# Slot 5's q and k turned by DMA instead of on TensorE, in a fused retention and feed-forward kernel

## The chip, the cores and the metric

The kernel runs on one core of one Trainium2 chip. The metric is the device time of one launch in microseconds. Engines: PE is TensorE (matmuls; PEld its weight loads), DVE is VectorE, ACT is ScalarE, POOL is GpSimd, SP is SyncE. SP and POOL issue DMAs here: POOL through a software queue (q0 in the profile), SP through a hardware queue (q1). Both queues run on the core's same 16 DMA engines.

## The reference

```python
# q, k, v: (4 batches, 8 heads, 768 steps, 64)
gamma = 1.0 - 2.0 ** (-5.0 - np.arange(H, dtype=np.float32))
for t in range(S):
    state = gamma[None, :, None, None] * state + np.einsum('bhd,bhe->bhde', k[:, :, t], v[:, :, t])
    y[:, :, t] = scale * np.einsum('bhd,bhde->bhe', q[:, :, t], state)
# x: y with heads beside each other, 3072 tokens x 512
h = x @ w_in                      # 512 -> 2048
out = (h * np.cos(h)) @ w_out     # 2048 -> 512
```

A linear recurrence with a decay for each head is followed by a feed-forward layer whose activation is h cos h. Inputs and output are float32; the matmuls run in bfloat16.

## The kernel before

**Tiles.** Time is cut into six chunks of 128 steps and the batches into two pairs, which gives 12 *slots* (`NP`), each one chunk of one batch pair, 256 tokens. Two slots make a *group* of 512 tokens for the feed-forward layer. For a slot the recurrence becomes matrix work:

1. q and k are cast to bfloat16 and multiplied by decay factors (`conv_q`, `conv_k`, `conv_v`: L323 to L346; for most slots q on POOL, k on ACT, v on POOL or DVE).
2. q and k are *transposed*, so that head dimension lies on the partitions (tile `qkt`, three buffers, slot p uses buffer p % 3).
3. Scores: k times q (`a_mm`/`a_one`, PE, L392), masked on DVE (`a_mask`, L411) into `am`.
4. Outputs: scores times v plus q times the running state; and the state's update (`y_block`, PE lines L483, L497, L511). From slot 4 on the scores of slot p+1 are woven into the block of slot p ("block 4" holds slot 4's outputs and slot 5's scores). Such a block takes six of the seven PSUM banks.
5. `y_copy` brings the outputs to `xt`, the feed-forward input; `s_copy` the state to `stb`.

The feed-forward layer comes in units of 4 or 8 matmuls, some 0.87 us of PE each: *half units* (`h_mm`, L614: 256 tokens, two column tiles of w_in), *full units* (`f_mm`, L593: 512 tokens, one column tile), each followed by a cosine on ACT (`f_cos`, L601) and a multiply on DVE (L605, L622), which frees the unit's bank; and *w_out units* (`o_mm`, L638), four of which make one 128-token output tile, copied by `o_out` and stored by SP.

**Transposes, two ways.** `t_mm` (L358 to L366) transposes on PE: for one slot 16 matmuls against an identity (L364), in two halves u, into PSUM; four copies (`t_copy`, L316 on ACT or L318 on DVE) bring them to `qkt`. `dma_t` (L351 to L353) does it with two DMA transposes on SP, q and k, 256 KB each, straight from `qs` and `ks` to `qkt`, without PE, PSUM or a copy. `DMA_T = 6` (L197) sets the border: slots 0 to 5 on PE, slots 6 and up by DMA.

**What sets the order.** Everything up to slot 6 is ordered by a planner at build time (class `Plan`). Each operation has a list of allowed engines, a cost, operations it comes after, and a rank; the planner goes through time, gives each free engine the ready operation of lowest rank, and so writes one fixed instruction order for each engine. It keeps counts of banks, cosine buffers, and a `port` token: POOL's two-input operations and some casts of DVE may not run at once. It models the loads as one queue (`mb`, `rate`, `lag`). The dictionary `SHIFT` adds to ranks and `ON` fixes engines, operation by operation (L168, L169); both come from a search. Where PE has nothing ready in the first 18 us, the planner inserts filler matmuls on zeros (`idle_mm`, L667). The plan's times only make the order: in the program each engine goes through its list and waits only for data and buffers. After slot 6 the order is a loop written out by hand.

The planner's entry for the DMA transposes stands at L803:

```python
            for w, x in enumerate("qk"):
                T["dt", p, w] = add("S", (1.3, 4.6), lambda e, p=p, w=w: dma_t(p, w),
                                    [T["c" + x, p, 0], T["c" + x, p, 1], ld["k", 7, 0]] + old, 10 * p,
                                    name="dt%d%d" % (p, w))
```

`ld["k", 7, 0]` is the load of slot 7's k, the last but one on POOL's queue: the plan places no DMA transpose before it has landed. `old` are the earlier users of the `qkt` buffer.

**Loads.** POOL issues, in a fixed list (`LOADS`), q, k and v of slots 1 to 7 (512 KB each; q4 is slot 4's q), the weights w_in in pieces (w0A to w3b) and w_out in four parts (o0 to o3, 1 MB read each). Slot 0's q goes over SP. From slot 8 on SP loads all. The order from q4 on: q4, o2, k4, v4, q5, k5, o3, v5, q6, k6, v6, q7, k7, v7.

Of the kernel before, what the change touches and what calls it, by code (L numbers as in the profile page):

```python
# [28 lines left out]
class Plan:  # L29
# [35 lines left out]
    def run(self, start, cold_until=0.0, look=0.0, fill=None, hold=""):  # L65
# [6 lines left out]
        t = 0.0  # L72
        while left:
            nxt = []
            for e in "SPADE":
# [6 lines left out]
                for op in left:  # L82
                    if e not in op["engines"]:
                        continue
                    r = self.ready(op)
                    if r is None:
                        continue
                    if r > t + 1e-9:
                        nxt.append(r)
                        coming.append((r, op["rank"]))  # L90
                        if op["rank"] < 20:
                            soon = min(soon, r)
                        continue
                    ok = True
                    for k, n in op["take"]:
                        tk = sorted(self.tokens[k])
                        n += op["spare"] if k == "bank" else 0
                        if len(tk) < n:
                            ok = False
                            continue  # L100

                        at = max(tk[n - 1] - 0.5, tk[n - 3]) if n > 5 else tk[n - 1]
                        if at > t + 1e-9:
                            nxt.append(at)
                            ok = False
                    if not ok:
                        continue
                    key = (op["rank"] + (0.5 if op["mode"] and op["mode"] != mode[0] else 0), op["n"])
                    if best is None or key < best[0]:
                        best = (key, op)  # L110
# [28 lines left out]
                for k, n in op["take"]:  # L139
                    self.tokens[k].sort()  # L140
                    del self.tokens[k][:n]
                op.update(eng=e, start=t, free=t + busy, done=t + took, lat=self.LAT[e])
                free[e] = t + busy
                if op["mb"]:
                    self.dma = max(self.dma, t + busy + 1.6) + op["mb"] / op["rate"] + op["lag"]
                    op.update(done=self.dma + 0.9, lat=0.0)
                for k, n in op["give"]:
                    self.tokens[k] += [op["done"] + 0.052] * n
# [19 lines left out]
SHIFT = {"ml010": 25.5, "mulf0.2": -74.7, "f0.3": 0.3, "cosf0.2": -11.6, "cosf0.3": -2.2, "mulf0.3": -4.9, "f0.2": 2.8, "m011": -20.0, "mulh1.4": -20.5, "m000": 82.7, "cosf0.5": -41.6, "ck21": 45.1, "a31": -124.5, "m100": 2.2, "f0.5": 23.0, "a5": -2.5, "v0": -97.2, "ms110": 6.4, "ml110": -41.8, "cosf0.4": -0.9, "f0.4": -9.8, "mulf0.5": 16.9, "eq51": 13.1, "m110": 64.4, "t20": -21.1, "k5": -46.0, "mulf0.8": 31.6, "yc21": -50.4, "f0.6": 2.1, "f0.7": 55.3, "ek10": -92.1, "w0b": -22.2, "a21": -34.2, "h1.0": 81.4, "cosh2.2": 3.0, "m501": 38.5, "yc30": -23.3, "ml011": -27.8, "mulf0.15": 5.8, "sc5": 79.1, "m201": -81.3, "mulh2.2": -18.0, "oc1": -45.8, "mulf0.14": -66.8, "cq31": -32.2, "mulf0.9": -47.9, "mulf0.6": 5.7, "cosf0.7": -27.8, "a30": -8.1, "cosf0.6": -7.2, "h0.2": -12.1, "eq21": -4.6, "cq51": 3.2, "cq41": 38.6, "f0.14": 23.8, "ek20": -13.4, "yc50": 39.8, "cv51": 23.4, "ek51": 88.5, "mulh2.10": 23.3, "cq70": 8.6, "f0.10": -46.0, "mulf0.13": 1.5, "h1.6": 5.9, "ml100": 20.1, "f0.15": 60.8, "o2.1": -8.1, "h3.10": 31.9, "t51": 14.8, "h3.0": -7.1, "h3.14": 28.8, "cq00": -2.7, "m601": 4.7, "h1.4": 1.8, "eq11": 37.0, "cosf0.12": -60.7, "v6": -26.4, "m400": 17.7, "mulh3.12": 67.0, "w2": 49.4, "sw": -53.6, "cv10": -0.0, "rv00": 14.5, "mulh2.8": 4.5, "ek50": 72.2, "cosf0.11": 2.4, "m101": -34.4, "h2.2": 1.1, "q2": -22.9, "q5": -59.7, "cosh3.14": 19.9, "y3": 19.8, "t40": 30.7, "o2": -0.8, "mulh3.4": -0.3, "cq40": -13.2, "mulh0.2": -29.3, "y5": -35.7, "mulh3.14": -25.5, "h2.12": -50.9, "oc0": -94.2, "a10": 39.9, "ek11": -35.3, "h0.6": 6.9, "eq40": -6.2, "h2.6": 58.1, "rv10": -9.1, "dt71": -1.3, "cosh3.8": -31.0, "cosh0.2": 18.8, "cv70": -67.6, "o3.1": -13.8, "cq60": -11.1, "ck60": 71.1, "m511": 10.9, "sc4": -15.9, "o1.3": -16.8, "m510": 4.5, "k4": 12.5, "h0.4": -9.2, "cq71": 3.6, "mulh3.2": 58.9, "cosh1.2": -26.7, "mulh3.6": -1.4, "cv61": 13.7, "o2.2": -9.8, "q6": -7.4, "o0.2": -7.5, "mulh2.4": 44.5, "mulh2.6": 22.6, "mulh3.10": 16.6, "v5": -53.7, "cq61": 27.8, "o1.1": -27.2, "ck61": 0.2, "m200": -10.8, "cosf0.9": 6.3, "cosh0.4": 11.6, "q4": 78.9, "cosh3.6": -6.8, "h1.2": -87.9, "tq01": 1.8, "oc3": -74.8, "mulh0.0": -16.9, "eq01": 11.2, "t21": 6.2, "ck41": 29.7, "cosh3.4": 9.3, "oc2": 8.6, "m211": 23.9, "cq01": -56.9, "w0a": 17.8, "o1.0": -7.7, "yc01": 2.2, "k7": 54.8, "yc51": -0.7, "cosf0.13": -14.9, "cosh2.10": -36.4, "yc00": 7.1, "cosh1.4": -13.4, "ek00": -8.7, "m611": -13.9, "tk10": -101.4, "mulh0.4": -40.7, "mulf0.10": 15.2, "m600": -35.2, "a00": -17.4, "cosh2.0": -5.5, "m301": 18.6, "rv11": -50.0, "sc0": -52.0, "ek01": -31.6, "cv01": 13.3, "ek21": -3.2, "cosf0.10": 7.2, "v7": -2.1, "ek40": 18.1, "t31": 22.7, "mulh1.6": 0.2, "eq30": -9.4, "y4": 19.2, "tk11": 1.9, "ek31": -26.9, "w3b": 23.5, "cosh2.12": -0.2, "cosh0.6": 4.7, "cosh2.8": -4.4, "cosh3.2": 25.8, "cv60": 2.7, "cosh2.4": -14.4, "v4": -1.1, "mulh2.12": 36.6, "dt61": -8.8, "eq41": -12.5, "mulf0.11": 31.8, "ek41": -0.8, "eq50": 9.1, "a11": -23.9, "yc10": 9.3, "o0.3": 0.3, "dt60": -3.3, "o3.3": 50.5, "mulh2.14": -42.3, "m610": -12.1, "f0.11": -0.6, "s0": 3.1, "cv11": 38.9, "h3.8": -17.4, "yc40": 14.3, "m410": -8.4, "h2.8": -4.0, "m300": 15.8, "o0": -14.6, "cv31": -27.4, "rv01": 0.6, "cosf0.14": 2.4, "cosh2.6": 11.7, "cv50": -6.8, "m010": -1.2, "ms011": -12.0, "f0.13": -5.2, "l8": 5.1, "ck70": 3.2, "t41": 1.0, "o1.2": -2.3, "cv71": 0.5, "tq11": 31.2, "h2.4": -3.6, "mulh0.6": 8.8, "t50": 7.1, "ck31": 42.7, "yc20": -52.3, "m001": -4.7, "y01": 62.0, "y2": 15.3, "f0.12": 20.5, "ms111": 2.0, "mulh1.2": -13.9, "cosh3.10": -49.0, "ck51": -9.0, "h0.0": -0.1, "eq31": 1.4, "eq20": -5.1, "q7": 1.5, "cosh3.0": 6.2, "cosh3.12": 1.5, "cv40": 2.3, "y11": 3.6, "o1": -24.4, "cv00": -1.4, "sc2": -3.2, "m411": 18.0, "m210": -8.1, "v3": 0.0, "eq10": 1.1, "tk01": 22.8, "yc41": -25.6, "cq21": -1.8, "f0.9": -31.4}  # L168
ON = {"cv70": "P", "cv00": "D", "cv30": "D", "cv31": "D", "cv60": "D", "cv11": "D", "cv10": "P", "rv01": "D", "sc5": "D", "rv11": "A", "yc20": "D", "sc3": "D", "eq40": "DA", "eq50": "A", "rv00": "A", "yc00": "D", "yc31": "DA", "ek51": "D", "ek11": "DA", "sc4": "D", "ek20": "A", "cv61": "P", "eq01": "DA", "cv51": "D", "ek41": "D", "eq41": "A", "cv20": "P", "yc01": "DA", "eq20": "A", "eq30": "DA", "ek50": "D", "ek00": "D", "sc2": "DA", "yc50": "DA", "yc40": "A", "yc21": "A", "cq21": "D", "ek40": "DA", "cv01": "D", "cv71": "P", "cv21": "P", "ek21": "DA", "cv41": "P", "cq20": "D", "ek10": "DA", "yc30": "A", "ek01": "D"}  # L169
# [4 lines left out]
def kernel(  # L174
# [22 lines left out]
    DMA_T = 6  # L197
# [515 lines left out]
    plan = Plan({"bank": 7, "cos": 3, "sem": 8, "out": 4, "port": 1, "ring": 7}, 6.5)  # L713
# [7 lines left out]
    ld["q", 0, 0], ld["q", 0, 1], ld["k", 0, 0], ld["k", 0, 1] = map(at, (3.9, 5.0, 7.4, 7.4))  # L721
    LOADS = ["Q1", "K1", "v0", "v1", "w0A", "w0B", "w0b", "w1a", "w1b", "w2", "q2", "k2", "w3a", "v2", "w3b", "o0", "q3", "k3", "v3", "o1", "q4", "o2", "k4", "v4", "q5", "k5", "o3", "v5", "q6", "k6", "v6", "q7", "k7", "v7"]
    LAG = {"w1b": 0.15}
    pend = []
    for i, x in enumerate(LOADS):
        if x[0] in "qkvQK":
# [3 lines left out]
                    [("sem", 1), ("ring", 1)], [("sem", 1), ("ring", 1)], mb=524288e-6, rate=330e-3, name=x)  # L730
# [3 lines left out]
        elif x[0] == "w":  # L734
# [4 lines left out]
                    mb=n * 2048e-6, rate=(415e-3 if n > 256 else 390e-3 if n > 128 else 370e-3),  # L739
# [3 lines left out]
        else:  # L743
            r = int(x[1])
            o = add("P", 0.76, lambda e, r=r: load_w_out(r), [("issued", prev)], 50 + i,
                    [("sem", 1)], [("sem", 1)], mb=1048576e-6, rate=415e-3, name=x)
# [4 lines left out]
    for p in range(PL + 2):  # L751
# [48 lines left out]
        else:  # L800
            for w, x in enumerate("qk"):
                T["dt", p, w] = add("S", (1.3, 4.6), lambda e, p=p, w=w: dma_t(p, w),
                                    [T["c" + x, p, 0], T["c" + x, p, 1], ld["k", 7, 0]] + old, 10 * p,  # L803
                                    name="dt%d%d" % (p, w))
# [115 lines left out]
    plan.run({"S": 2.5, "P": 3.2, "A": 5.5, "D": 3.6, "E": 4.2}, COLD, 0.6, (4.2, 18.0, 0.225, lambda e: idle_mm(e, 2)), HOLD)  # L920
# [80 lines left out]
```

## Time and profile before

| | |
|---|---|
| median of 3 runs | 208.82 us (208.31 to 208.92) |
| span of the profiled execution, first to last instruction | 206.6 us |
| the profiled execution's own device time | not listed; the median is 2.2 us above the span |
| PE matmuls | 201.9 us busy, 2179 instructions |
| DVE, ACT, POOL busy | 112.9, 115.1, 75.2 us |
| 16 transposes of slot 5 on PE (L364) | from 55.38 us, 0.89 us in the chain |
| filler matmuls (L667) | 35, 11.2 us |
| first DMA transpose issued on SP | 62.56 us |
| landing after issue of the 12 DMA transposes | 2.7 / 2.8 / 4.4 us (min, median, max) |

Times in the text are microseconds from the span's start. PE time is modelled from the ends of pipelined matmuls. The chain of work that ended last is followed back from the end: what is in it set the time. A load's landing is counted from the start of its issue. Of the software queue's loads, these matter below (start of issue, landing after it, and so the time of landing):

| load | issued | lands after | at |
|---|---|---|---|
| w_out part o0 | 21.47 | 11.1 | 32.57 |
| k5 | 36.38 | 13.9 | 50.28 |
| k6 | 45.18 | 12.1 | 57.28 |
| k7 | 50.76 | 11.0 | 61.76 |
| v7 (the last) | 51.95 | 11.4 | 63.35 |

### The profile page before, as it was taken

What the parts mean: (1) busy time and instruction counts of PE and PEld (TensorE: products, weight loads), DVE (VectorE), ACT (ScalarE), POOL (GpSimd) and SP (SyncE); (2) the same over time, 40 slices, a digit from 0 to 9 for tenths busy, and PEclk for the clock granted to TensorE, in tenths of its full rate; (3) what the DMA queues carried; (4) which work ended last, traced back from release to release, by engine and by line L of the source; (5) the groups of instructions that cost most, each with busy time, mean ns of one, the idle gap of its engine ahead of it and who ended that gap; (6) DMA issues with size and microseconds to landing.
All of it is one profiled execution on the core that took longest, in us unless ns stands there. A gap on an engine that the chain in (4) does not pass through costs nothing.

```text
span 206.6 us, 5235 instructions
## 1 busy us (share of the span) xinstructions
PE 201.9 (98%) x2179; PEld 108.9 (53%) x2179; DVE 112.9 (55%) x194; ACT 115.1 (56%) x193; POOL 75.2 (36%) x79
## 2 busy tenths in 40 slices
PE   7999999999999999999999999999999999999994
PEld 2547665868945545445445445445444444444442
DVE  5477899776787548338438438448442444444000
ACT  7566794859965357547547546554555553554120
POOL 8899989799985003305206105200000000000000
PEclk9999999999999999999999999999999999999999
DMA  6999999999999865886876975501101101110212
GB/s 117 172 264 201 304 242 322 252 333 278 341 332 190 199 156 150 206 210 155 190 183 157 144 198 147 156 0 56 53 1 51 51 3 51 51 51 0 105 52 102
DMA packets 59656, 32.15 MB, mean 156 GB/s; under 512 B 48752, under 2 KB 54128, under 8 KB 59632
## 3 DMA queue, kind: packets, MB, share of 16 engines
q0 software_dynamic: 15408, 15.47, 34.6%
q1 hardware_dynamic: 44080, 16.28, 31.7%
q8 instruction: 17, 0.28, 0.6%
q10 hardware_dynamic: 144, 0.07, 0.1%
q14 instruction: 7, 0.06, 0.1%
HBM read 27.26 MB, written 6.29 MB: 162 GB/s over the span
## 4 chain that ended last, share of the span: by engine, by line
PE 93%; DMA 4%; POOL 1%; issue 0%; DVE 0%; POOLq 0%; DVEq 0%
PE bank L638 39%; PE bank L593 30%; PE bank L614 10%; DMA kx<-in_k_dram 4%; PE bank L392 2%; PE bank L483 2%; PE bank L364 2%; PE bank L658 2%; PE st_ps L511 2%; PE bank L667 2%; PE bank L497 1%; POOL ks L284 1%; PE bank L434 1%; POOL qs L284 1%; PE bank L402 0%
## 5 line engine op out<-in xcount | busy, mean ns | idle before, releaser
L601 ACT ACTIVATE cosb<-bank,halfpi 128x512 bf16<-128x512 f32 x96 | 65.6, 689 | 54.1 <-PE bank L593 47.8
L638 PE MATMUL bank<-w_out_sb,gt 128*128 128x512 bf16 x368 | 91.0, 379 | 0.0
L605 DVE TENSOR_TENSOR gt<-bank,cosb 128x512 bf16<-128x512 f32 x72 | 49.1, 689 | 55.7 <-ACT cosb L601 55.7
L593 PE MATMUL bank<-xt,w_in_sb 128*128 128x512 bf16 x288 | 73.2, 379 | 0.0
L638 PEld LDWEIGHTS <-gt 128*128 128x128 bf16 x368 | 35.5, 98 | 42.3 <-DMA w_out_sb<-in_moe_w_out_dram 0.3
L593 PEld LDWEIGHTS <-w_in_sb 128*128 128x128 bf16 x288 | 27.5, 98 | 32.3
L327 POOL TENSOR_TENSOR qs<-qf,gq 128x512 bf16<-128x512 f32 x18 | 18.5, 1046 | 42.4 <-PE bank L483 32.0
L411 DVE TENSOR_TENSOR am<-bank,mask 128x512 bf16<-128x512 f32 x40 | 24.8, 681 | 3.5 <-PE bank L392 3.5
L316 ACT COPY ob<-bank 128x512 f32<-128x512 f32 (+1 forms) x24 | 14.0, 582 | 16.0 <-PE bank L638 13.9
L614 PE MATMUL bank<-xt,w_in_sb 128*128 128x256 bf16 x192 | 22.4, 273 | 0.0
L614 PEld LDWEIGHTS <-w_in_sb 128*128 128x128 bf16 x192 | 18.6, 98 | 3.3 <-DVE xt L318 0.3
L622 DVE TENSOR_TENSOR gt<-bank,cosb 128x512 bf16<-128x512 f32 x24 | 16.2, 689 | 5.6 <-ACT cosb L601 5.4
L316 ACT CAST xt<-bank 128x512 bf16<-128x512 f32 x21 | 11.4, 588 | 10.6 <-PE bank L483 10.5
L316 ACT CAST ks<-kf 128x512 bf16<-128x512 f32 x20 | 11.5, 623 | 1.9 <-DMA kf<-in_k_dram 1.9
L667 PE MATMUL bank<-zero 128*128 128x512 bf16 x35 | 11.2, 449 | 1.1 <-DVE halfpi L683 1.1
L483 PE MATMUL bank<-am,vs 64*64 64x128 bf16 (+1 forms) x320 | 10.3, 206 | 0.1
L334 POOL TENSOR_TENSOR vs<-vf,gk 128x512 bf16<-128x512 f32 x8 | 8.2, 1043 | 6.0 <-DMA vf<-in_v_dram 3.8
L284 POOL DMA_DIRECT2D vf<-in_v_dram x8 | 9.4, 1178 | 1.9 <-DVE vs L339 1.4
L339 POOL TENSOR_TENSOR vs<-vf,gk 128x512 bf16<-128x512 f32 x8 | 8.7, 1096 | 2.5 <-PE bank L483 1.3
L318 DVE CAST stb<-st_ps 128x512 bf16<-128x512 f32 x9 | 6.2, 689 | 3.4 <-PE st_ps L511 2.6
L483 PEld LDWEIGHTS <-vs 64*64 64x64 bf16 x320 | 7.8, 107 | 0.5 <-POOLq L531 0.2
L392 PE MATMUL bank<-qkt 64*64 64x128 bf16 (+1 forms) x320 | 7.9, 206 | 0.0
(66 smaller groups left out, 131.7 us busy)
## 6 DMA issues: line engine op xcount, KB each, us to landing
out_dram<-ob SPq DMA_DIRECT2D x23, 256.0 KB, 2.5
vf<-in_v_dram POOLq DMA_DIRECT2D x8, 512.0 KB, 11.7
qf<-in_q_dram POOLq DMA_DIRECT2D x6, 512.0 KB, 12.3
kf<-in_k_dram POOLq DMA_DIRECT2D x6, 512.0 KB, 12.1
w_out_sb<-in_moe_w_out_dram POOLq DMA_DIRECT2D x4, 512.0 KB, 14.1
qf<-in_q_dram SPq DMA_DIRECT2D x4, 512.0 KB, 4.8
w_in_sb<-in_moe_w_in_dram POOLq DMA_DIRECT2D x5, 256.0 KB, 8.5
kf<-in_k_dram SPq DMA_DIRECT2D x16, 64.0 KB, 3.1
```

The costliest lines, as they stand in the source:

```text
L284: eng.dma_start(out=t.rearrange("p b h d -> p (b h) d"), in_=src[ds(2 * bp, 2), :, ds(c * C, C), :].rearrange("b h t d -> t (b h) d"))
L316: nc.scalar.copy(out=out, in_=in_)
L327: ENG[e].tensor_tensor(out=qb(p)[:, b], in0=qf[p % PRE][:, b], in1=bc(gq, ORDER[p] % NC), op=ALU.mult)
L411: nc.vector.tensor_tensor(out=am[p % 2][b][u], in0=bank.rearrange("p (a t) -> p a t", a=HP), in1=(dec[:, b] if p < 2 else mask[second(p, 0 ...
L483: m = nc.tensor.matmul(held["yp", p][b][ts(j, 64), a, lo:], lhsT=vs[p % NB][ts(r, 64), b, h, :], rhs=am[p % 2][b][h // 4][ts(r, 64), h % 4 ...
L593: nc.tensor.matmul(bank, lhsT=w_in_sb[:, i, ts(f, 128)], rhs=xt[g % 2][:, i, :], start=(i == 0), stop=(i == KIN - 1))
L601: nc.scalar.activation(out=cb, in_=bank, func=AF.Sin, bias=halfpi)
L605: nc.vector.tensor_tensor(out=gt[g % 2][:, f, :], in0=bank, in1=cb, op=ALU.mult)
L614: nc.tensor.matmul(bank[:, ts(e, 256)], lhsT=w_in_sb[:, i, ts(f + e, 128)], rhs=xt[g % 2][:, i, ts(hf, 256)], start=(i == 0 and e == 0), s ...
L622: nc.vector.tensor_tensor(out=gt[g % 2][:, f : f + 2, ts(hf, 256)], in0=bank.rearrange("p (f t) -> p f t", f=2), in1=cb.rearrange("p (f t) ...
L638: nc.tensor.matmul(bank, lhsT=gt[g % 2][:, f, ts(j, 128)], rhs=w_out_sb[:, f, :], start=(f == 0), stop=(f == KOUT - 1))
L667: nc.tensor.matmul(bank[:, : 256 * n].rearrange("p (n t) -> p n t", n=n), lhsT=zero[:, :128], rhs=zero.unsqueeze(1).to_broadcast([128, n, ...
```

## The change

`DMA_T` goes from 6 to 5: slot 5's q and k are transposed by two DMA transposes on SP instead of by 16 matmuls on PE and four copies. For slot 5 the plan does not wait for slot 7's k, takes 5.6 us for a transpose instead of 4.6, and adds 1.1 us to its model of the load queue for each. No load is held back for them. In the planner an operation that is put on ACT no longer takes the `port` token. Some figures of the planner's load model are changed (rates, lags, landing of the first loads, ACT's start). `SHIFT` and `ON` are new throughout; `ON` has 32 entries instead of 47. The hand-written part after slot 6 is as before. Lines after L197 move by 8 to 10 in the changed file: L364 becomes L372, L392 L400, L483 L491, L614 L622, L638 L646, L353 L361, L667 L675.

```diff
@@ class Plan, run: the checks, takes and gives of tokens
                     for k, n in op["take"]:
+                        if k == "port" and e == "A":
+                            continue
...
                 if op["mb"]:
                     self.dma = max(self.dma, t + busy + 1.6) + op["mb"] / op["rate"] + op["lag"]
                     op.update(done=self.dma + 0.9, lat=0.0)
+                elif op["lag"]:
+                    self.dma = max(self.dma, t + busy) + op["lag"]
...
-SHIFT = {"ml010": 25.5, ...
-ON = {"cv70": "P", ...
+SHIFT = {"Q1": -19.5, ...
+ON = {"cv00": "D", ...
...
-    DMA_T = 6
+    DMA_T = 5
...
-    plan = Plan({"bank": 7, "cos": 3, "sem": 8, "out": 4, "port": 1, "ring": 7}, 6.5)
+    plan = Plan({"bank": 7, "cos": 3, "sem": 8, "out": 4, "port": 1, "ring": 7}, 6.78)
...
-    LAG = {"w1b": 0.15}
+    LAG = {"w1a": 0.45, "w3b": -0.15, "v2": 0.15, "o1": 0.6}
...
-                T["dt", p, w] = add("S", (1.3, 4.6), lambda e, p=p, w=w: dma_t(p, w),
-                                    [T["c" + x, p, 0], T["c" + x, p, 1], ld["k", 7, 0]] + old, 10 * p,
-                                    name="dt%d%d" % (p, w))
+                T["dt", p, w] = add("S", (1.3, 5.6 if p < 6 else 4.6),
+                                    lambda e, p=p, w=w: dma_t(p, w),
+                                    [T["c" + x, p, 0], T["c" + x, p, 1],
+                                     ld["k", 7, 0] if p > 5 else None] + old, 10 * p,
+                                    lag=1.1 if p < 6 else 0.0, name="dt%d%d" % (p, w))
...
-    plan.run({"S": 2.5, "P": 3.2, "A": 5.5, "D": 3.6, "E": 4.2}, COLD, ...
+    plan.run({"S": 2.5, "P": 3.2, "A": 6.6, "D": 3.6, "E": 4.2}, COLD, ...
```

In the program that this gives, as far as the order of instructions tells: the loads keep their order on POOL. On PE all is in the same order from slot 2's first w_out unit to the end of block 3. Between block 3 and block 4 stand now nine half units, slot 4's transposes in two parts, slot 4's scores and three w_out units; before, nine half units, the transposes of slots 4 and 5, slot 4's scores and five w_out units. The two w_out units come after block 4. On SP the two new transposes stand ahead of the first output store. On POOL the multiplies of q5 move ahead of the last issues: the first before k7's, the second before v7's. On ACT the two casts of k6 stand ahead of the cosine of the last half unit but one before block 4.

## The prediction

> **What bounds the kernel now.** I read the page's busy shares first, then the slices, then the chain of work that ended last.
>
> ```profile
> span 206.6 us, 5235 instructions
> PE 201.9 (98%) x2179; PEld 108.9 (53%) x2179; DVE 112.9 (55%) x194; ACT 115.1 (56%) x193; POOL 75.2 (36%) x79
> PE   7999999999999999999999999999999999999994
> DMA  6999999999999865886876975501101101110212
> PE 93%; DMA 4%; POOL 1%; issue 0%; DVE 0%; POOLq 0%; DVEq 0%
> ```
>
> PE is the bound: 98% busy, 93% of the chain. After the first 16 us it has no hole in any slice, so a PE instruction taken out of the stretch from 16 us on is worth its full time, unless PE then arrives somewhere too early. The DMA row matters as well: full in slices 1 to 12 (5 to 67 us), while the loads of GpSimd's queue stream in. In the same chain in order of time, around slot 5's transposes (L364), the columns are start, length, what:
>
> ```profile
> 47.56 1.00 PE bank L364 x16
> 48.56 6.99 PE bank L614 x64
> 55.55 0.89 PE bank L364 x16
> 56.44 0.87 PE bank L614 x8
> 57.31 0.86 PE bank L638 x4
> 58.18 0.56 PE bank L392 x26
> 58.74 3.56 PE bank L638 x16
> 62.30 0.15 PE st_ps L511 x2
> ```
>
> The 0.89 us at 55.55 is slot 5's. At 62.30 starts the block that holds slot 4's outputs and slot 5's scores (below: block 4).
>
> **The sum, part by part.** Profiled span 206.6; the median of the runs shown is 208.82, so 2.2 us lie around the span, and I leave them unchanged.
>
> *Removed from PE:* 16 transposes, 0.89 us on the path. Four copies out of PSUM go too (two on ACT at about 0.53 us a step, two on DVE at 0.39): both engines are 55% busy there, so these gain nothing by themselves.
>
> *Fillers and start:* the changed program has 35 filler matmuls (L667 before), as now; PE's 32 fewer rows are just the transposes and their weight loads. Before the first w_out unit PE has the same list (8 half units, 8 full ones, slot 2) in another order, and that unit is held by its load (issued 21.47, 11.1 us to landing: 32.57; it runs at 32.81). A start a few tenths earlier or later ends there: 0, bounds -0.3 and +0.3. From there to the end of block 3 (47.56) the PE order is the same.
>
> *Moved on PE:* after block 3 come seven half units (0.874 each), slot 4's transposes (0.89, now in two parts), w_out 0.86, slot 4's scores 0.56, w_out 0.86, half unit 0.87, w_out 0.86, half unit 0.87, then block 4. 47.56 + 6.12 + 0.89 + 0.86 + 0.56 + 0.86 + 0.87 + 0.86 + 0.87 = 59.45. Before it stood at 62.30: 0.89 less for the transposes, two w_out units put behind it. So block 4 asks for its inputs 2.85 us earlier, with all loads in the same order. That is the second half of the change.
>
> *Added on SP:* two DMA transposes (k, then q) of 256 KB. Their inputs: the last cast of k5 on ACT, which I place at 52.2 (k5 lands at 36.38 + 13.9 = 50.28; the casts alternate with cos), and the second multiply of q5 on POOL, at 53.0 (now ahead of v7's load). SP is free, so issues at 52.3 and 53.65 (1.24 to 1.34 us each). Behind them on SP stand two output stores and slot 6's transposes, which have over 4 us of slack. What their own transfer costs the DMA engines, I read from a later one that runs alone (98 to 99.2 us):
>
> ```profile
> DMA packets 1047, 0.26 MB, mean 216 GB/s; under 512 B 1047, under 2 KB 1047, under 8 KB 1047
> q1 hardware_dynamic: 1047, 0.26, 96.1%
> ```
>
> About 1,024 packets of 256 B; the engines are full for about 0.95 us. It lands 2.7 to 4.4 us after issue in this trace, but never beside a full software queue. Beside it a 256 KB store (59.58) took 4.4 us instead of 2.5. With 4.4 + 1.9 the second transpose lands at about 53.65 + 6.3 = 59.95, against slot 5's scores at 59.45 + 0.4 = 59.85: nearly free. Bounds: 2.7 (never waited for) and, if one row passes per load packet, until the loads are through (first rival).
>
> *What the loads pay.* At 52 to 58 us the software queue already fills all 16 engines (DMA share 1.01 to 1.06, 343 GB/s in the stretch 54 to 58). At 11.5 to 13 us small SP transfers run beside it:
>
> ```profile
> q0 software_dynamic: 150, 0.47, 95.6%
> q1 hardware_dynamic: 155, 0.03, 11.4%
> ```
>
> 0.47 MB in 1.5 us is 313 GB/s: 155 small packets cost the loads 9%. Engine time is shared out, not spare. So the transposes push every load behind them by up to 2 x 0.95 = 1.9 us. The one that matters is k6: issued 45.18, landing 12.1 later, at 57.28. In the changed ACT order the two casts of k6 (1.03 us together before the next can start) stand *ahead of* the cos of the half unit that ends at 57.7; then cos and then DVE's multiply, 0.69 each and 0.72 with the handover, which frees a PSUM bank; block 4 takes six of the seven banks, and that bank is among them. With k6 at 57.28: 57.28 + 1.03 + 0.72 + 0.72 = 59.75, just in time for 59.9. **There is no slack: every microsecond that k6 comes later is a microsecond of PE.** With k6 at 57.28 + 1.9 = 59.2 the bank is free at 61.65, and PE waits 61.65 - 59.9 = 1.75 us. Bounds: 0 (the loads lose nothing) and 2.4 (both transposes at the longest issue-to-landing seen).
>
> *The port rule and the new shift tables* move casts among ACT, DVE and POOL (state copies of slots 2 to 5 to ACT) and cost no instruction. The one that could bite, slot 4's state copy on ACT behind the casts of k7 (61.76, or 63.7 delayed), is done by 65.4; block 5 starts at 67.9 or later. Cover gone, it would cost what k7 exceeds 66.
>
> Sum: -0.89 + 1.75 = +0.86; 206.6 + 0.9 = 207.5 span, 208.82 + 0.86 = **209.7 us**.
>
> **A rule weighed.** The row above has 155 hardware packets to 150 software packets: one to one. The Trainium skill (DMA: Bandwidth & Descriptors, "Queues, rings and completion order") says that each DMA engine goes round its queues packet by packet and drains a whole packet, typically 9 to 17 descriptors, before it switches. If a transpose's 64 rows per engine travel 16 to a packet, that is four turns, the transposes are early and only the loads pay, the sum above; if each row is a packet of its own, as the row's small transfers were, the first rival comes. No run here shows which holds for a transpose.
>
> **Rivals.**
> 1. *Transposes starved, much slower.* One 256 B row per 4 KB load packet: a load packet takes 0.19 us of an engine (343 GB/s over 16), so 64 rows take over 12 us, and in fact until the queue is empty. The last load lands at 51.95 + 11.4 = 63.35; with what the rows add, about 64; then 0.95 us each for what is left: second landing near 65.6. PE stands from 59.9 to 65.6: -0.89 + 5.7 = +4.8, 213.6. For: the one-to-one row. Against: those were copies of four to eight descriptors per engine, and a transpose alone is steady at full rate. It decides once fewer than about four rows pass per turn: at four, 32 turns of 0.19 us and 1.9 us of their own from 52.7 on (issue and, I assume, 0.4 us) end near 60.7, and landing takes about 1 us more. By the Trainium skill (TensorE: Matmul & The Clock Gate, "Part 1") PE falls to half clock after some 3.4 us idle and takes as long to recover; an estimate from that page is 1.7 us more, 215.3, which I leave out of the sum. The trace shows only the start's cold matmuls: seven fillers in 3.17 us, 0.45 each, against 0.23 later.
> 2. *It does what it says, faster.* The transposes slip between load packets, k6 is no later than about 0.5 us, and the 0.89 is kept: 207.9. For: loads q7, k7 and v7 still landed 1.5 to 1.6 us apart with the 256 KB store beside them. Against: that store met only the queue's tail, and DMA was full before.
> 3. *Break-even:* k6 late by 0.9 us, 208.8. It is the edge between the sum and rival 2, not a case of its own.
>
> **Chances.** The sum (PE waits 1 to 2.4 us in block 4, 208.9 to 210.4): 0.45. Rival 2: 0.35. Rival 1 with milder forms of it: 0.20. I forecast 209.7. The range 207.5 to 212.5 takes in rival 2 with its start bound and the milder half of rival 1. About 0.3% (0.6 us) is what a measurement of this kernel can tell from no change. Faster by more than that: 0.28 from rival 2 and 0.02 from the sum's low end, 0.30. Within: 0.07 + 0.11 = 0.18. Slower: 0.32 + 0.20 = 0.52.
>
> **What would show it.** In the profile after: PE's waits in block 4 (L392/L483 group near 59 to 62 us) with a bank's or ACT's release, k6's landing nearer 59 than 57.3, and the two early transposes landing 4 to 6.5 us after issue: the sum. PE waiting for a DMA on qkt until 64 us or more: rival 1. No PE hole after 16 us and k6 at 57.3 to 57.8: rival 2. I would be wrong in the working if PE waits anywhere ahead of block 4, or if slot 6's transposes hold block 5.

## The result, and the profile after

The changed kernel takes 215.41 us (median of 6 runs, 214.9 to 218.38) against 208.87 us for the kernel before on the same chip: a ratio of 1.030, 95% interval 1.028 to 1.033. Some executions are slow as a whole (one of these six, one of experiment 7's ten and four of experiment 9's six); the ratios and intervals leave those out, the medians do not, and without its slow one the changed kernel's median is 215.21 us. It is slower by 6.3 to 6.5 us and lies above the forecast range; it is the first rival that came, with the clock's share.

From the page of the changed kernel: the span, the busy times, three rows of its 40 slices (5.3 us each) and the chain's shares.

```profile
span 213.3 us, 5171 instructions
PE 201.6 (95%) x2139; PEld 109.1 (51%) x2163; DVE 111.4 (52%) x189; ACT 116.0 (54%) x194; POOL 74.9 (35%) x79
PE   8999999999927999999999999999999999999993
PEclk9999999999985999999999999999999999999999
DMA  7999999999999366776696986611011101110212
PE 82%; DMA 9%; issue 2%; POOL 2%; ACT 2%; DVE 1%; DVEq 0%; POOLq 0%; ACTq 0%
```

PE has as many busy microseconds as before, though 16 transposes are gone. Counted from 0, there is a hole in slices 11 and 12 (59 to 69 us), the granted clock drops in the same two, and DMA, 4% of the chain before, has 9%. Which transfer that is, the chain in order of time says (start, length, what):

```profile
45.81 8.48 DMA vf<-in_v_dram
54.30 10.63 DMA qkt<-qs
64.93 0.14 issue
...
66.52 0.57 PE bank L491 x8
67.09 0.54 PE bank L646
67.63 0.22 issue
67.86 7.51 PE bank L646 x30
75.36 0.15 PE st_ps L519 x2
```

The transpose of slot 5's q, issued at 54.30, lands at 64.93. (That slot 6's v released it, as the first row has it, is inferred by the profile and does not hold: by its own entry v6 landed at 58.6, and this issue followed the end of the one before it on SP, at 54.18.) PE began block 4 at 59.35, did what needs nothing of slot 5, and stood from 59.95 to 65.06: 5.11 us. The list of PE's waits gives it one entry (engine and line, releaser: total, times, longest):

```profile
PE bank L400 <- DMA qkt<-qs: 5.1, 1, 5.1
```

SP's own queue shows the two issues of slot 5 and what stood behind them (start, length, line, operation):

```profile
51.95 2.23 SPq L361 DMA_TRANSPOSE qkt<-ks  x1
54.30 6.31 SPq L361 DMA_TRANSPOSE qkt<-qs  x1
60.69 1.01 SPq L658 DMA_DIRECT2D out_dram<-ob  x2
61.81 2.31 SPq L361 DMA_TRANSPOSE qkt<-qs  x1
```

An issue took 1.23 to 1.97 us before, most of them 1.24 to 1.34; the second one here keeps SP for 6.31 us. The packets of the two queues in the stretch from 58 to 60 us (packets, MB, share of the 16 engines' time) give the reason:

```profile
q0 software_dynamic: 172, 0.62, 95.2%
q1 hardware_dynamic: 172, 0.04, 10.2%
```

172 to 172: one row of 256 bytes (0.04 MB over 172) for every load packet, most of them of 4 KB. The start and end of each packet in the same trace show that the two really take turns, one by one and not in batches: 171 of the 172 rows start 3 to 9 ns before a load packet ends, and all 172 load packets 3 to 9 ns before a row ends, where packets that had nothing to do with each other would fit so in some 28%. From 54 to 56 us not one row passed, though the first transpose was issued at 51.95. From 62 to 64 us, as the last load lands (63.56), it is 957 to 24.

The clock in the stretches 62 to 63, 63 to 64, 64 to 66, 66 to 68, 68 to 70 and 70 to 72 us (after the five engines' busy times: granted clock, DMA share, GB/s):

```profile
62.00:63.00 1.00, 0.00 (x0) 0.00 (x0) 0.00 (x0) 0.00 (x0) 0.44 (x1) 0.89 1.43 137
63.00:64.00 1.00, 0.00 (x0) 0.00 (x0) 0.00 (x0) 0.00 (x0) 0.00 (x0) 0.50 1.08 174
64.00:66.00 2.00, 0.94 (x47) 0.97 (x50) 0.03 (x1) 0.00 (x0) 0.00 (x0) 0.50 1.13 363
66.00:68.00 2.00, 1.78 (x42) 1.28 (x33) 2.00 (x4) 1.23 (x3) 0.77 (x1) 0.50 1.80 286
68.00:70.00 2.00, 2.00 (x6) 0.67 (x6) 2.00 (x3) 1.37 (x3) 1.27 (x2) 0.60 0.61 70
70.00:72.00 2.00, 2.00 (x11) 0.92 (x10) 0.42 (x1) 0.00 (x0) 0.00 (x0) 1.00 0.58 131
```

A mean of 0.89 from 62 to 63 is half clock from about 62.8 on, 2.8 us into PE's wait; a mean of 0.60 from 68 to 70 is half clock until about 69.6, 4.5 us after PE went on. The eight w_out units behind block 4 (five before; two came from ahead of the block, one from behind block 5) take 8.27 us (67.09 to 75.36) where eight at 0.86 us make 6.9.

### The profile page after: what moved, and what is told of

Same layout as the page of the kernel before. It is cut to its first block, busy times and chain, and to the rows that moved or that the text cites. A ratio compares the mean times of both kernels' runs of the same rounds, so it can differ in the third digit from the quotient of the medians.

```text
span 213.3 us, 5171 instructions
## 1 busy us (share of the span) xinstructions
PE 201.6 (95%) x2139; PEld 109.1 (51%) x2163; DVE 111.4 (52%) x189; ACT 116.0 (54%) x194; POOL 74.9 (35%) x79
## 2 busy tenths in 40 slices
DMA packets 61768, 32.67 MB, mean 153 GB/s; under 512 B 50864, under 2 KB 56240, under 8 KB 61744
## 4 chain that ended last, share of the span: by engine, by line
PE 82%; DMA 9%; issue 2%; POOL 2%; ACT 2%; DVE 1%; DVEq 0%; POOLq 0%; ACTq 0%
PE bank L646 36%; PE bank L601 27%; DMA qkt<-qs 5%; PE bank L622 5%; PE bank L675 4%; DMA vf<-in_v_dram 4%; PE bank L400 2%; PE bank L491 2%; PE bank L666 2%; PE st_ps L519 1%; PE bank L372 1%; ACT cosb L609 1%; PE bank L505 1%; DVE gt L613 1%; PE bank L442 1%
## 5 line engine op out<-in xcount | busy, mean ns | idle before, releaser
L646 PE MATMUL bank<-w_out_sb,gt 128*128 128x512 bf16 x358 | 91.1, 383 | 1.0 <-issue 0.4
L601 PE MATMUL bank<-xt,w_in_sb 128*128 128x512 bf16 x274 | 71.2, 380 | 0.6 <-issue 0.2
L646 PEld LDWEIGHTS <-gt 128*128 128x128 bf16 x368 | 35.8, 98 | 43.2 <-issue 1.8
L622 PE MATMUL bank<-xt,w_in_sb 128*128 128x256 bf16 x192 | 22.6, 273 | 0.1
L622 PEld LDWEIGHTS <-w_in_sb 128*128 128x128 bf16 x192 | 18.4, 98 | 3.4 <-DVE xt L326 0.2
L400 PE MATMUL bank<-qkt 64*64 64x128 bf16 (+1 forms) x320 | 8.7, 213 | 5.3 <-DMA qkt<-qs 5.1
L675 PE MATMUL bank<-zero 128*128 128x512 bf16 x35 | 10.8, 438 | 1.1 <-DVE halfpi L691 1.1
L491 PE MATMUL bank<-am,vs 64*64 64x128 bf16 (+1 forms) x320 | 11.0, 212 | 0.1
L400 PEld LDWEIGHTS <-qkt 64*64 64x64 bf16 x320 | 7.3, 112 | 6.7 <-DMA qkt<-ks 5.2
L491 PEld LDWEIGHTS <-vs 64*64 64x64 bf16 x320 | 8.4, 110 | 0.5 <-POOLq L539 0.2
```

The lines of the kernel that those rows point to most:

```text
L400: return nc.tensor.matmul(ap[b][ts(x, 64), a, lo:], lhsT=kt(p % NB, b, h)[:, ts(x, 64)], rhs=qt(p % NB, b, h)[:, lo:], tile_position=(64 * ...
L491: m = nc.tensor.matmul(held["yp", p][b][ts(j, 64), a, lo:], lhsT=vs[p % NB][ts(r, 64), b, h, :], rhs=am[p % 2][b][h // 4][ts(r, 64), h % 4 ...
L601: nc.tensor.matmul(bank, lhsT=w_in_sb[:, i, ts(f, 128)], rhs=xt[g % 2][:, i, :], start=(i == 0), stop=(i == KIN - 1))
L622: nc.tensor.matmul(bank[:, ts(e, 256)], lhsT=w_in_sb[:, i, ts(f + e, 128)], rhs=xt[g % 2][:, i, ts(hf, 256)], start=(i == 0 and e == 0), s ...
L646: nc.tensor.matmul(bank, lhsT=gt[g % 2][:, f, ts(j, 128)], rhs=w_out_sb[:, f, :], start=(f == 0), stop=(f == KOUT - 1))
L675: nc.tensor.matmul(bank[:, : 256 * n].rearrange("p (n t) -> p n t", n=n), lhsT=zero[:, :128], rhs=zero.unsqueeze(1).to_broadcast([128, n, ...
```

## The experiments

Theory A: *the transposes are starved*. They are issued into DMA engines that the software queue keeps full, get one row for each load packet, and are through only when the queue has ended; all the rest (PE's wait, the clock) follows from that. Its rivals stand in the expectations. Nine kernels were run, each beside the kernel before on the same chip.

**1. The new order without the DMA.** Everything of the change but the transposes' place:

```diff
-    DMA_T = 5
+    DMA_T = 6
```

> The new plan with all its tables, but slot 5 transposed on PE again. Theory A (the whole loss is the two transposes that let one 256 B row pass for each packet of the load queue, plus the slow PE clock after the wait): no DMA wait in block 4, the 16 transposes cost their 0.89 us, PE without a hole after 16 us, so 208.3 to 209.2 us, as before. Rival B (the new order costs time of its own, because block 4 comes 2.85 us earlier and the casts of k6 stand ahead of a cos): slower than 210 us, with PE waits in block 4 for a bank. Rival C (the new order is itself better, and hid part of the loss): under 208.2 us.

Measured: 209.06 us (12 runs), ratio 1.001 (1.000 to 1.003), span 207.3, clock 1.00, no DMA among PE's waits. The new tables, the port rule and the new load figures are worth nothing that can be measured, either way. The whole loss belongs to the DMA.

**2. A shorter queue.** The last three loads, slot 7's q, k and v, are not issued:

```diff
-            o = add("P", 1.2, lambda e, p=p, n=x[0]: load(nc.gpsimd, p, n),
+            o = add("P", 1.2, lambda e, p=p, n=x[0]: load(nc.gpsimd, p, n) if p < 7 else None,
```

> The changed kernel without the loads of slot 7's q, k and v: slot 7 then works on slot 2's old data, so part of the input is left out. The software queue ends with v6, near 58.6 us instead of 63.6. Theory A: the transposes end about 1.5 us after the last load, so the second lands near 60 to 60.7 instead of 64.9, PE waits under 1 us in block 4, the clock stays up, 207.9 to 209.2 us. Rival D (a transpose issued while loads run takes 10 to 12 us of its own, whatever is queued): landing stays near 62 to 65, 212 us or more.

Measured: 209.19 us (one run), span 207.4. The last load (slot 6's v, issued 45.99, 12.6 to landing) is through at 58.6. PE's wait and SP's queue:

```profile
PE bank L400 <- DMA qkt<-qs: 0.7, 1, 0.7
```

```profile
52.42 2.00 SPq L361 DMA_TRANSPOSE qkt<-ks  x1
54.54 3.88 SPq L361 DMA_TRANSPOSE qkt<-qs  x1
```

The second transpose lands at 61.00 (theory A had 60 to 60.7), 6.46 us after issue instead of 10.63. The same two transposes, issued within half a microsecond of the changed kernel's, come some 2.4 us after the queue's end in this kernel, and 1.4 us after it there (63.56, 64.93). From 58 to 60 us the hardware queue passed 1,635 packets to the loads' 2. The transposes themselves are not slow; the queue's end sets them.

**3. The wait filled.** 25 filler matmuls of the kernel's own kind stand in PE's order ahead of block 4, to keep the clock up while the transposes are as late as before:

```diff
+        if p == 4:
+            for i in range(25):
+                nc.tensor.matmul(
+                    banks.free_list[0].rearrange("p (n t) -> p n t", n=2), lhsT=zero[:, :128],
+                    rhs=zero.unsqueeze(1).to_broadcast([128, 2, 256]), start=True, stop=True)
```

> The changed kernel with 25 filler matmuls on zeros (5.4 us of PE) put ahead of block 4, where PE stood idle. Theory A with its second part (5.2 us of wait, then about 2.4 us because PE's granted clock is 0.5 from 63 to 69 us): landing unchanged near 64.9, clock 1.0 throughout, 212.6 to 213.4 us. Rival E (the clock plays no part, all 6.5 us are wait and order): 215 us or more.

Measured: 214.14 us (4 runs), ratio 1.025 (1.023 to 1.028), between the two expectations. The fillers run from 60.05 to 65.53, and all of block 4 comes behind them. Slot 5's scores begin at 65.92, in the changed kernel at 65.06, which had done the first part of block 4 ahead of its wait. So this kernel is 0.86 us behind it there. The stretches from 60 to 65 and from 65 to 70 us, first of the changed kernel, then of this one (PE's busy time is the second figure, the granted clock the third from the end):

```profile
60.00:65.00 5.00, 0.00 (x0) 0.00 (x0) 0.00 (x0) 0.20 (x1) 2.04 (x2) 0.78 1.18 262
65.00:70.00 5.00, 4.71 (x81) 2.91 (x83) 4.03 (x6) 2.60 (x5) 2.04 (x2) 0.54 1.18 214
```

```profile
60.00:65.00 5.00, 5.00 (x25) 2.29 (x24) 1.13 (x2) 0.69 (x1) 2.04 (x2) 1.00 1.26 244
65.00:70.00 5.00, 4.71 (x127) 2.84 (x127) 3.41 (x6) 2.60 (x5) 2.04 (x2) 1.00 1.47 202
```

In the same 4.71 busy microseconds PE does 127 matmuls instead of 81 (38 small ones of block 4 were done ahead of the wait there). The slow clock's price is that 0.86 us and what this kernel gains to the end: 0.9 us between the spans (1.8 us in all), 1.07 between 215.21 and 214.14 (1.9 us). Here too the packets were one to one from 58 to 60 us, 173 to 173, and took turns one by one, with a filled PE: the starvation has nothing to do with PE.

**4. Four loads held back, behind both transposed slots.** v6, q7, k7 and v7 are issued only after a one-column copy on POOL has read slot 5's and slot 6's transposed tiles; slot 6's transposes no longer wait for k7:

```diff
+    GATE = [2, 0]
...
-                                     ld["k", 7, 0] if p > 5 else None] + old, 10 * p,
+                                     None] + old, 10 * p,
...
+    g = add("P", 0.15, lambda e: [nc.gpsimd.tensor_copy(out=pad, in_=qkt[i][:, 1, 7, 127:])
+                                  for i in GATE],
+            [T["dt", p, w] for p in (5, 6) for w in range(2)], -9e3, name="gate")
+    for o in plan.ops:
+        if o["name"] == "v6":
+            o["after"].append(g)
```

> The changed kernel with the last four loads (v6, q7, k7, v7) held back: on POOL they stand behind two copies of one column each that read slot 5's and slot 6's transposed tiles, so they start after those transposes have landed; the plan no longer waits for k7 with slot 6's transposes. Theory A: the queue is empty from about 56 us, slot 5's transposes land by 59.5, block 4 does not wait, slot 6's land by 64, the held loads land 66 to 71, in time for block 6 at 76.7; 207.6 to 208.4 us, faster than before by the 0.89 us of the PE transposes or a little less. Rival D: still 212 us or more. Rival F (the held loads come too late for slot 7): PE waits in block 6, 209 to 212 us.

Measured: 212.75 us (6 runs), ratio 1.020 (1.016 to 1.023). Block 4 had no wait. But the held loads went out from 65.3 us on, k7 landed at 75.58 and slot 7's transposes at 79.65, and PE waited in block 6:

```profile
PE bank L400 <- DMA qkt<-ks: 2.1, 1, 2.1
```

Theory A's half of it holds (the stall at block 4 goes with the queue); the hold was too long, and rival F moved the wait two blocks down, at a price above its 209 to 212 us. That wait of 2.1 us cost the clock as well: it is at half from 81.2 to 84.7 us, some 1.7 us of work. The two are enough for the 3.4 us that the profiled run (212.25) lies over the kernel before.

**5. The old order with the DMA.** The kernel before, its tables, rates and port rule, with only this:

```diff
-    DMA_T = 6
+    DMA_T = 5
...
-                                    [T["c" + x, p, 0], T["c" + x, p, 1], ld["k", 7, 0]] + old, 10 * p,
+                                    [T["c" + x, p, 0], T["c" + x, p, 1], ld["k", 7, 0] if p > 5 else None] + old, 10 * p,
```

> The tables, rates and rules of the plan of before are kept, and only the one thing is changed: slot 5 goes by DMA, without the wait for slot 7's k. Theory A (the two transposes are starved by the loads behind which they are issued, whatever the plan): the software queue still ends near 63.5 us, the second transpose lands at 64 to 65.5, PE stands some 4 to 5.5 us ahead of block 4 and its clock drops; the profile 211.5 to 213.5 us, the time 213.5 to 216. Rival C' (the annealed plan brought it about, by issuing the transposes at a bad moment): a wait under 2 us, time under 211.

Measured: 215.3 us (4 runs, 213.59 to 216.63), ratio 1.031 (1.026 to 1.036). The packets from 58 to 60 us, then PE's wait:

```profile
q0 software_dynamic: 170, 0.62, 95.6%
q1 hardware_dynamic: 169, 0.04, 11.2%
```

```profile
PE bank L392 <- DMA qkt<-qs: 5.5, 1, 5.5
```

The same ratio and nearly the same wait in another order. With experiment 1 this separates the two halves of the change cleanly: the order is worth 0.1%, the DMA costs 3%, and neither needs the other.

**6. Smaller load packets.** The five last loads are each cut into one load for either half of the batch:

```diff
-            o = add("P", 1.2, lambda e, p=p, n=x[0]: load(nc.gpsimd, p, n),
+            o = add("P", 1.2, lambda e, p=p, n=x[0], i=i: load(nc.gpsimd, p, n + "0 " + n + "1" if i > 28 else n),
```

> The changed kernel, with the five last loads (k6, v6, q7, k7, v7) each cut into two of half the batch, so that their packets are 2 KB instead of 4 KB; bytes and order are the same. Theory A (the rings take turns packet by packet, one row of 256 bytes for each load packet): while both are under way the two queues' packets stay one to one, and both rise to some 300 in 2 us (172 each in the changed kernel from 58 to 60 us); the transposes then land before the queue has ended, the second by about 62 us, unless POOL issues the loads later. Rival G (the transposes have a fixed share of the time or of the bytes): their rows stay near 172 in 2 us, and only the loads' packets double. The time may go either way, since POOL has ten loads to issue in the place of five: 209 to 216.

Measured: 221.81 us (2 runs), ratio 1.063 (1.058 to 1.068). The edit did not do what it was meant to. The five loads together have 80 packets more than before, not twice as many (the page counts 61,848 in all instead of 61,768), and the 80 are packets of 4 bytes, so the data still travels in 4 KB. Rival G falls by the changed kernel's own trace all the same: 20 of its 172 load packets from 58 to 60 us have 4 bytes, the others 4 KB, and each of the 20 has a row right before it and right behind it, as each large one has. So it is the turns that are shared out, and neither time nor bytes. What the edit did was to spread the queue out. Between the ten issues POOL waited and did other work, and the last half load was issued at 58.5 and landed 14.3 us later, at 72.8. Slot 5's q was issued late as well:

```profile
57.61 0.02 issue
57.63 14.96 DMA qkt<-qs
72.59 0.14 issue
```

It landed at 72.59, 0.2 us ahead of the last load, and PE waited 11.3 us. That looks like theory A once more, a longer queue and a later transpose, but it is not a clean case: from 60 to 62 us 341 hardware packets passed beside 43 load packets, and the engines moved only 115 GB/s. Why both were slow there is open.

**7. The hold, behind slot 5 alone.** As experiment 4, but the gate reads slot 5's tile only, and slot 7's transposes wait for k7 again:

```diff
-    GATE = [2, 0]
+    GATE = [2]
...
-                                     None] + old, 10 * p,
+                                     ld["k", 7, 0] if p > 6 else None] + old, 10 * p,
...
-            [T["dt", p, w] for p in (5, 6) for w in range(2)], -9e3, name="gate")
+            [T["dt", p, w] for p in (5,) for w in range(2)], -9e3, name="gate")
```

> As e4 (slot 6's v and slot 7's three loads are issued only when slot 5's transposed tile is there), but not held for slot 6's transposes as well, and slot 6's transposes don't wait for them; slot 7's transposes wait for slot 7's k again. Theory A: slot 5's transposes run beside a queue that ends near 57 us and land by 59.5, no wait ahead of block 4; the four loads are issued from 59.5 to 64 and land by 68. Slot 6's transposes, issued at 58 and 60, meet a queue that is nearly empty at first: they land by 65 to 67.5, block 5 waits at most 1 us; slot 7's are issued near 67 and land by 72. Profile 206.2 to 207.5, time 208 to 209.2. Rival F' (slot 6's transposes are starved in their turn until the four held loads are through, at 68 to 69): PE waits 1 to 3 us ahead of block 5 and the time is 210 to 212.5.

Measured: 209.71 us (10 runs), ratio 1.005 (1.004 to 1.007), over theory A's 208 to 209.2. No DMA wait ahead of blocks 4 or 5, clock 1.00; slot 6's transposes were not starved, since they were issued before the held loads had filled the engines. PE lost 1.0 us at block 5's banks to an output copy on ACT, and ACT's timeline shows what that copy stood behind (start, length, line, operation; in brackets the idle time before it and its releaser):

```profile
62.02 0.60 ACT L324 CAST stb<-st_ps 128x512 bf16<-128x512 f32 x1
69.30 0.62 ACT L324 CAST ks<-kf 128x512 bf16<-128x512 f32 x1 [6.68 <-DMA kf<-in_k_dram]
69.82 0.58 ACT L324 COPY ob<-bank 128x512 f32<-128x512 f32 x1
```

ACT waited 6.68 us for k7, now late, with a finished bank queued behind the cast.

**8. And slot 7's k cast on POOL.**

```diff
-                T["ck", p, b] = add("A", SB2, lambda e, p=p, b=b: conv_k(p, b, e),
+                T["ck", p, b] = add("A" if p < 7 else "P", SB2 if p < 7 else TT, lambda e, p=p, b=b: conv_k(p, b, e),
```

> As e7, and slot 7's k is cast on POOL instead of ACT. In e7 ACT stood 6.7 us at the first of these casts, with two copies of finished output banks behind it, and PE lost 1.0 us at block 5's banks. Theory A with H (that 1.0 us is all that is left of the hold's price): no wait of over 0.3 us ahead of blocks 4, 5 and 6, the profile near 207.0 us (e7's 208.0 less 1.0), the time 208.4 to 208.9, which is 0.3 us under e1's at best. Rival (the held loads are late for something else too: slot 7's transposes, or block 5's values): a wait of 1 us or more moves to block 6 or stays, time 209.4 to 211.

Measured: 208.47 us (12 runs), ratio 0.9985 (0.9967 to 1.0003), span 206.5, clock 1.00. SP's queue shows the pair of slot 5, then PE's waits, none of them for a DMA:

```profile
50.61 1.34 SPq L361 DMA_TRANSPOSE qkt<-qs  x1
52.35 4.83 SPq L361 DMA_TRANSPOSE qkt<-ks  x1
```

```profile
PE bank L675 <- DVE halfpi L691: 1.1, 1, 1.1
PE bank L400 <- DVE qkt L326: 0.3, 1, 0.3
PE bank L646 <- DVE gt L630: 0.2, 1, 0.2
```

They land 7.6 and 6.8 us after issue, 0.9 and 1.8 us after the queue's last load ahead of the gate (k6, at 57.3), and before the gate at 59.62. Against the kernel before, the changed kernel is at 1.030, experiment 1 at 1.0012 and this one at 0.9985: 3% under the first, and 0.27% or 0.6 us under the second, of the 0.89 us that the transposes take on PE. The last two intervals overlap (0.9997 to 1.0026 for experiment 1), so this 0.6 us is likely and not shown. Against the kernel before it is at the edge of what can be told from no change.

**9. The same hold in the old order.** The tables of before, with the gate and the cast of experiment 8.

> The tables of before with slot 5 by DMA, with e8's hold (slot 6's v and slot 7's loads are issued only when slot 5's tile is there, slot 7's k is cast on POOL). Theory A: no stall ahead of block 4, the clock stays at 1.00, so the 5 to 7 us of e5 go; what stays is the saving of PE's 16 transposes, 0.89 us, less what the hold costs: 207.6 to 209.0. Rival: the old order has no room for the hold (its loads are issued later than the order expects, engines wait in their order for them): 209.5 to 212.

Measured: ratio 1.018 (1.013 to 1.023), from two of the 6 runs; all 6 lie as far apart as 211.7 and 220.8 us, so the size is uncertain, the sign is not. In the profile (span 209.9) no DMA is among PE's long waits. The held v6 is issued at 60.65 and lands at 68.2, block 5's state comes late, and PE is busy 17.5 of the 20 us from 60 to 80. So the hold works in the new order and not in this one: it needs an order that has room for it.

## Why the prediction was wrong, point by point

**Removed and moved on PE: right.** Block 4 was placed at 59.45; it began at 59.35. (The two causes named for its 2.85 us, the transposes and two w_out units, make 2.6; the rest was not named.)

**The port rule, the tables, the start: right.** The tables were put at 0, the start at 0 with bounds of 0.3 us; experiment 1 has the order at 0.1% (0.2 us).

**Added on SP: this step failed.** It had the second transpose land 4.4 + 1.9 us after its issue, at 59.95, nearly free. It landed 10.63 us after, at 64.93, and PE waited 5.11 us. The 4.4 came from a store of 256 KB beside the queue's tail, which moved no packet before 60.5 us, when the loads were running out; the 1.9 came from the engine time of the two transposes. Neither row shows what a stream of 256-byte rows gets beside a *full* queue. One row did show that, and the prediction had printed it: 155 hardware packets to 150 software packets. It was then set aside because the transfers of that row were small. The trace after has 172 to 172, experiments 3 and 5 have 173 to 173 and 169 to 170. And where the prediction let the rows start 0.4 us behind an issue, the first moved at 56.13, 4.2 us after it. The rule weighed there (the Trainium skill, DMA: Bandwidth & Descriptors, "Queues, rings and completion order") agrees that the engines go round packet by packet; its typical 9 to 17 descriptors for a packet did not hold for a transpose's rows, of which each took a turn of its own.

**What the loads pay: wrong by nearly all of it.** k6 was to land at 59.2, 1.9 us late, and to cost PE 1.75 us. It landed at 57.0, ACT cast it at once, and no bank was waited for. The term was no fair trial for k6, since the first row moved only at 56.13 and 59 rows had passed by 57. But the loads behind it paid little too: q6 landed 0.25 us earlier than in the kernel before (55.43), v7 0.2 us later (63.56), so they lost some 0.5 us over those 8 us, not 1.9. This is the other face of the same error. Engine time is shared out, as the prediction said, but who pays is decided by the size of the packets: of two queues that take turns, the one with 4 KB packets loses little (0.62 MB in 2 us instead of the 0.67 of 52 to 54 us, 7%), the one with 256 B waits. The sum let the transposes be early *and* the loads pay for them.

**The first rival: right in mechanism and nearly in size.** It had the second landing at 65.6 (64.93), PE's wait at 5.7 us (5.11), and 213.6 us. The rest is the clock, which it left out of its sum: 1.8 to 1.9 us by experiment 3. The rule it cited (the Trainium skill, TensorE: Matmul & The Clock Gate, "Part 1": some 3.4 us idle to half clock, as long to recover) agrees in kind, with 2.8 us of wait to half clock and 4.5 us of work to full clock measured here. The rule does not foresee experiment 4, where the half clock came 1.6 us after a wait of only 2.1 us. An estimate from that page was 1.7 us, and 213.6 + 1.7 is 215.3, against a measured 215.2 to 215.4. So close a sum is in part luck: its wait is some 0.5 us too long, and 0.7 to 0.8 us of the loss below stand in none of its terms.

**The chances.** That rival had 0.20, and the range took in its milder half only. What could have told it apart was in the trace of before. In the row of 155 to 150 the packets alternate one by one as well: 153 of the 155 start 3 to 9 ns before a load packet ends (58% would by chance), though by the prediction's account those transfers had four to eight descriptors for each engine. Taken over to a transpose, 64 turns of a full queue at 0.19 us are 12 us, where some 6 us were to spare.

From before to after, the span adds up as follows. Block 4 begins 2.95 us earlier with two w_out units (1.72 us) moved behind it: -1.23. The wait: slot 5's scores begin 5.71 us after block 4 instead of 0.39 (as in experiment 3), +5.3. The slow clock: +1.8 to +1.9. That is +5.9 to +6.0 of the measured +6.7. The remaining 0.7 to 0.8 us was not traced to a place; the spans of the kernel before alone, over all its runs, lie between 206.3 and 207.9 us.

## What to carry to other kernels

A DMA whose packets are small costs little beside a queue whose packets are large, and, as here, it can wait for nearly all of that queue: count turns, not bytes, and ask when the big queue ends, not how much bandwidth is left. If such a transfer must go early, what worked here was to hold back the loads that have slack until it has landed, and then every in-order engine that handles those loads has to be looked at for work queued behind them. A small gain on the bound engine (0.4% here) is not worth a transfer that can make it stop for long enough to lose its clock.

## What the runs showed of the hardware that was not expected

Beside a full software queue the first row of a transpose moved some 4 us after its issue (issued 51.95, first row at 56.13; 3.1 to 4.3 us in the other runs), against some 1.2 us where the engines were free (issued 98.22, rows from 99.4 in the kernel before). So the turns begin late as well.

A second transpose behind a starved one keeps its issuing engine: 6.31 us on SP in the changed kernel, 3.88 with the shorter queue, against 1.24 to 1.34 for most issues when the engines are free. The output stores and the next slot's transposes stood behind it; they had the slack here.

POOL casts a 128x512 half of k in 0.61 us (experiment 8), as fast as ACT (0.62), though its multiplies of that shape take 1.04.
